# Two-level Strassen products in the first channel layer of the last batch

## The chip, the cores and the metric

The kernel runs on one NeuronCore of a Trainium2 chip. The metric is the device time of one execution in microseconds. Engine names are those of the profile: PE multiplies matrices, PEld loads its weights, DVE is VectorE, ACT is ScalarE, POOL is GpSimd, SP is SyncE, which issues nearly all DMAs.

## The reference

Inputs q, k and v have 4 batches, 8 heads, 768 positions and 64 columns a head. A sparse attention block makes x of 4 x 768 x 512, and this follows:

```python
X = np.fft.fft(x, axis=1)
X = np.fft.fft(X, axis=2)
u = x + np.real(X).astype(np.float32)
mu = np.mean(u, axis=-1, keepdims=True)
var = np.mean((u - mu) ** 2, axis=-1, keepdims=True)
un = (u - mu) / np.sqrt(var + 1e-06)
ch = np.maximum(un @ w_ch1, 0.0) @ w_ch2      # 512 -> 2048 -> 512
return (u + ch).astype(np.float32)
```

The change concerns `un @ w_ch1` of the last batch: 768 x 512 times 512 x 2048, all in float32.

## The kernel before

The program goes through the batches one after the other. For batch b it runs two channel layers and, beside them, the attention and the Fourier stage of batch b + 1. The last batch (b = 3) has nothing beside its channel layers: they are the last 145 us.

**Layer one** (`gen_hidden`, matmuls at L1377) makes the hidden activations in 16 tiles of 128 rows, taken in eight pairs j = 0 to 7. Rows of pair j come from the two halves of the hidden dimension, so a pair is a 2 x 2 block product: two tile rows, two halves of 384 positions, and a contraction over 512 that is cut in two halves of 256. It is done with Strassen's scheme in Winograd's form: seven products instead of eight. Each product contracts over 256, which is two matmuls (kk = 0, 1) of 384 columns. So a pair takes 14 matmuls. The seven left operands of a pair (A11, A12, S3, A22, S1, S2, S4) lie ready in DRAM as `dw1[j]` and come by `get_w1` into the three buffers of tag w1; the seven right operands (`u`, indices B11, T3, B21, B22, T1, T2, T4) are made on chip by `_right_sums` once per batch. Products go to three PSUM banks X, Y, Z (the profile's hx, hy, hz). ACT copies the first of each output block to h in SBUF (L1388, L1394, L1396), DVE adds the others (L571 is the helper `tt`), and a ReLU follows (DVE at L1383 for b > 0, ACT at L1407 for the last block).

**Layer two** (`gen_out`, matmuls at L1446) works in the same way on strips of 128 positions. Four left sums S1 to S4 are made by DVE from h (the profile's tile s), the right operands `dw2[j]` come by `get_w2`, and DVE adds the products ox, oy, oz to x. Each layer is cut in two parts, c = 0 and 1: four pairs in layer one, then a layer-two pass over these four (three strips i = 0 to 2), then the other four.

PSUM has eight banks: four of the tag "bank" (Fourier stage and channel layers) and four of the tag "attn" (attention).

**Order.** Generators yield after each piece, and `drive` takes pieces from several of them in turn. The program's instructions are then put on the engines' queues by priority, which is mostly program order; `tc.issue_after(mark)` puts an instruction behind a given one on its engine. Each engine works through its queue strictly in order, waiting at each instruction for what it needs. A buffer is reused when its readers are done.

The lines at which the last batch's channel layers begin are:

```python
most = chain(gen_hidden(b, 0), gen_out(b, 0), gen_hidden(b, 1))
...
drive((most, 44, 0), (gen_attention(b + 1) if b + 1 < B else iter(()), 80, 0))
last = gen_out(b, 1)
if b + 1 < B:
    drive((gen_fourier(b + 1), 22, 600), (last, 12, 0))
else:
    drive((last, 1, 0))
```

Of the kernel before, what the change touches and what calls it, by code (L numbers as in the profile page):

```python
# [9 lines left out]
FP = mybir.dt.float32  # L10
I32 = mybir.dt.int32
U32 = mybir.dt.uint32
AF = mybir.ActivationFunctionType
ALU = mybir.AluOpType
AX = mybir.AxisListType

P = 128
# [401 lines left out]
QB = 64  # L419
# [69 lines left out]
def _main_program(ctx, tc, q, k, v, moe_w_ch1, moe_w_ch2, out):  # L489


    nc = tc.nc
    B, H, S, D = q.shape
    DM = H * D
# [54 lines left out]
    def fetch(out, in_):  # L549

        ins = nc.sync.dma_start(out=out, in_=in_)
        if in_order[0]:
            tc.keep_in_program_order(ins)
        return ins.ins

    def abank(shape, name):
        return psum.tile(shape, FP, tag="attn", bufs=4, name=name)

    def bank(shape, name):
        return psum.tile(shape, FP, tag="bank", bufs=4, name=name)  # L560
# [9 lines left out]
    def tt(out, in0, in1, op):  # L570
        return nc.vector.tensor_tensor(out=out, in0=in0, in1=in1, op=op).ins  # L571
# [28 lines left out]
    def room(name):  # L600
        return bpool.tile([P, NC * 2 * S], FP, tag="room", name=name)
# [622 lines left out]
    def gen_fourier(b):  # L1224
# [117 lines left out]
        for t in range(NST):  # L1342
            half, i = divmod(t, HT)
            if b:
                normalise(half, i)
            ps = bank([P, 2, 2, P], f"unt_{b}_{t}")
            with tc.issue_after(marks[("av", 1, 0) if half else ("sc", 1, 0)]) if b == 0 else ExitStack():
                for d in range(NDT):
                    nc.tensor.transpose(ps[:, d // 2, d % 2, :], un[:, t, P * d:P * (d + 1)], ident)  # L1349
            ins = (nc.vector.tensor_copy if t % 2 and (b or half) else nc.scalar.copy)(  # L1350
                out=u[:, half:half + 3:2, :, P * i:P * (i + 1)], in_=ps)
            if t == NST - 1:
                marks["u"] = ins.ins
            yield
        _right_sums(tt, u.rearrange("p a k n -> p a (k n)"))
        wt["u", b] = u

    def gen_hidden(b, c):
        u = wt["u", b]
        js = range(NC * c, NC * (c + 1))  # L1360
        h = wt["h", b] = bpool.tile([P, NC, 2, S], FP, tag="h", name=f"h_{b}_{c}")
        for j in js:
            if 0 < j < NJ - 2:
                get_w1(b, j + 2)
            if (b, c) != (1, 0):
                get_w2(b, j)
            else:
                for i in ((0, 1), (2,), (3,), ())[j]:
                    get_w2(b, i)
            w = wt[1, b, j]  # L1370
            c11, c12 = h[:, j - NC * c, 0, 0:S2], h[:, j - NC * c, 0, S2:S]
            c21, c22 = h[:, j - NC * c, 1, 0:S2], h[:, j - NC * c, 1, S2:S]
            X, Y, Z = (bank([P, S2], f"h{n}_{b}_{j}") for n in "xyz")

            def product(ps, a, r, start, stop):
                for kk in range(2):
                    ins = nc.tensor.matmul(ps, w[:, a, kk, :], u[:, r, kk, :], start=start and kk == 0,  # L1377
                                           stop=stop and kk == 1, skip_group_check=True)
                marks["hidden", b] = ins.ins

            def relu(t):
                if b:
                    nc.vector.tensor_scalar(out=t, in0=t, scalar1=0.0, scalar2=None, op0=ALU.max)  # L1383
                else:
                    nc.scalar.activation(out=t, in_=t, func=AF.Relu)

            product(X, A11, B11, True, False)
            nc.scalar.copy(out=c11, in_=X)  # L1388
            product(Y, A12, B21, True, True)
            marks["dense"] = tt(c11, Y, c11, ADD)  # L1390
            some_sums(3 if (b, c) == (1, 0) and j else 0)
            yield
            product(X, S2_, T2, False, False)
            nc.scalar.copy(out=c12, in_=X)  # L1394
            product(Z, S1, T1, True, False)
            nc.scalar.copy(out=c22, in_=Z)  # L1396
            relu(c11)
            some_sums(3 if (b, c) == (1, 0) and j else 0)
            yield
            product(X, S3, T3, False, False)  # L1400
            marks["dense"] = tt(c22, X, c22, ADD)
            product(Z, S4, B22, False, True)
            marks["dense"] = tt(c12, Z, c12, ADD)
            some_sums(3 if (b, c) == (1, 0) and j else 0)
            yield
            product(X, A22, T4, False, True)
            nc.scalar.activation(out=c21, in_=X, func=AF.Relu)  # L1407
            relu(c22)
            relu(c12)
            issued.add(("h", b, j))  # L1410
            some_sums(3 if (b, c) == (1, 0) and j else 0)
            yield

    def gen_out(b, c):
        x, h = x_of[b], wt["h", b]
        js = range(NC * c, NC * (c + 1))
        if (b, c) == (0, 0):

            for t in range(NST):
                ps = bank([P, DM], f"o_{b}_{c}_{t}")  # L1420
                for n, j in enumerate(js):
                    for hf in range(2):
                        nc.tensor.matmul(ps, h[:, n, hf, P * t:P * (t + 1)], wt[2, b, j][:, 2 * hf:2 * hf + 2, :],  # L1423
                                         start=(n, hf) == (0, 0), stop=(n, hf) == (NC - 1, 1))
                    if n % 2 == 0:
                        yield
                tt(x[:, t, :], ps, x[:, t, :], ADD)
            issued.add(("o", b, c))
            return
        for i in range(HT):  # L1430
            t1, t2 = slice(P * i, P * (i + 1)), slice(S2 + P * i, S2 + P * (i + 1))
            left = {A11: h[:, :, 0, t1], A12: h[:, :, 1, t1], A22: h[:, :, 1, t2]}
            for s in (S1, S2_, S3, S4):
                left[s] = bpool.tile([P, NC, P], FP, tag="s", bufs=5, name=f"s{s}_{b}_{c}_{i}")
            a21 = h[:, :, 0, t2]
            tt(left[S1], a21, left[A22], ADD)
            tt(left[S2_], left[S1], left[A11], SUB)
            tt(left[S3], left[A11], a21, SUB)
            tt(left[S4], left[A12], left[S2_], SUB)
            X, Y, Z = (bank([P, HD], f"o{n}_{b}_{c}_{i}") for n in "xyz")  # L1440
            x11, x12 = x[:, i, 0:HD], x[:, i, HD:DM]
            x21, x22 = x[:, HT + i, 0:HD], x[:, HT + i, HD:DM]

            def product(ps, a, r, start, stop):
                for n, j in enumerate(js):
                    nc.tensor.matmul(ps, left[a][:, n, :], wt[2, b, j][:, r, :], start=start and n == 0,  # L1446
                                     stop=stop and n == NC - 1, skip_group_check=True)

            product(X, A11, B11, True, False)
            marks["dense"] = tt(x11, X, x11, ADD)  # L1450
            product(Y, A12, B21, True, True)
            marks["dense"] = tt(x11, Y, x11, ADD)
            yield
            product(X, S2_, T2, False, False)
            marks["dense"] = tt(x12, X, x12, ADD)
            product(Z, S1, T1, True, False)
            marks["dense"] = tt(x22, Z, x22, ADD)
            yield
            product(X, S3, T3, False, False)
            marks["dense"] = tt(x22, X, x22, ADD)  # L1460
            last = (b, c, i) == (B - 1, 1, HT - 1)
            if last:
                fetch(out=out[b, P * (HT + i):P * (HT + i + 1), HD:DM], in_=x22)
            product(Z, S4, B22, False, True)
            marks["dense"] = tt(x12, Z, x12, ADD)
            if last:
                fetch(out=out[b, P * i:P * (i + 1), :], in_=x[:, i, :])
            yield
            product(X, A22, T4, False, True)
            marks["dense"] = tt(x21, X, x21, ADD)  # L1470
            if NC * (c + 1) == NJ and not last:
                for t in (i, HT + i):
                    fetch(out=out[b, P * t:P * (t + 1), :], in_=x[:, t, :])
            elif last:
                fetch(out=out[b, P * (HT + i):P * (HT + i + 1), 0:HD], in_=x21)
            if i == HT - 1:
                issued.add(("o", b, c))
            yield


# [31 lines left out]
    def chain(*gens):  # L1512
        for gen in gens:
            yield from gen
# [51 lines left out]
    for b in range(B):  # L1566


        most = chain(gen_hidden(b, 0), gen_out(b, 0), gen_hidden(b, 1))
        if b == 0:  # L1570
            in_order[0] = False
            drive((most, 5, 0), (weights, 10, 0), (attn, 1, 0))
# [2 lines left out]
            drive((most, 44, 0), (gen_attention(b + 1) if b + 1 < B else iter(()), 80, 0))  # L1575
        last = gen_out(b, 1)
        if b + 1 < B:
            drive((gen_fourier(b + 1), 22, 600), (last, 12, 0))
        else:
            drive((last, 1, 0))  # L1580
# [53 lines left out]
```

## Time and profile before

| what | value |
|---|---|
| median of three runs | 793.5 us (792.02 to 793.65) |
| profiled execution, its own time | 790.53 us |
| its span in the profile | 788.6 us |
| PE busy | 776.1 us, 98% of the span |
| mean granted PE clock | 0.999 |
| last batch, layer one, c = 0 | 638.9 to 675.2 us |
| last batch, layer two, c = 0 | 675.2 to 711.5 us |
| last batch, layer one, c = 1 | 711.5 to 747.6 us |
| last batch, layer two, c = 1 | 747.6 to 784.4 us |

The profile describes one execution; its times are microseconds from the start of the span, and the execution takes about 2 us more than the span. A float32 matmul of the program appears as two records of PE and two weight loads of PEld. A line of a group of instructions names source line, engine, operation, output<-inputs, shapes and count; then busy time and mean duration in ns; then the idle time of the engine ahead of them and what ended it. A table by stretches gives the busy time of each engine in a stretch, with the number of instructions, the granted clock, the DMA share and GB/s.

### The profile page before, as it was taken

What the parts mean: (1) busy time and instruction counts of PE and PEld (TensorE: products, weight loads), DVE (VectorE), ACT (ScalarE), POOL (GpSimd) and SP (SyncE); (2) the same over time, 40 slices, a digit from 0 to 9 for tenths busy, and PEclk for the clock granted to TensorE, in tenths of its full rate; (3) what the DMA queues carried; (4) which work ended last, traced back from release to release, by engine and by line L of the source; (5) the groups of instructions that cost most, each with busy time, mean ns of one, the idle gap of its engine ahead of it and who ended that gap; (6) DMA issues with size and microseconds to landing.
All of it is one profiled execution on the core that took longest, in us unless ns stands there. A gap on an engine that the chain in (4) does not pass through costs nothing.

```text
span 788.6 us, 14351 instructions
## 1 busy us (share of the span) xinstructions
PE 776.1 (98%) x5920; PEld 562.9 (71%) x5920; DVE 491.2 (62%) x1017; ACT 224.1 (28%) x491; POOL 49.2 (6%) x87
## 2 busy tenths in 40 slices
PE   9999999999999999999999999999999999999997
PEld 6778455445588866787578866788569865886686
DVE  5899978697889566652759545552667623533352
ACT  3565656236536022100236012200136012001200
POOL 0000000000000030200310020300220000000000
PEclk9999999999999999999999999999999999999999
DMA  9999887796855279965442169611513163106001
GB/s 214 184 266 237 206 275 196 242 260 221 232 161 155 49 231 261 204 103 177 154 144 87 54 209 212 184 55 31 223 44 134 54 220 134 47 0 234 0 28 57
DMA packets 133353, 121.82 MB, mean 154 GB/s; under 512 B 94464, under 2 KB 114912, under 8 KB 133088
## 3 DMA queue, kind: packets, MB, share of 16 engines
q1 hardware_dynamic: 132160, 118.53, 53.9%
q0 software_dynamic: 576, 2.10, 0.8%
q8 instruction: 48, 0.79, 0.4%
q10 hardware_dynamic: 544, 0.20, 0.1%
q14 instruction: 25, 0.20, 0.1%
HBM read 97.22 MB, written 23.59 MB: 153 GB/s over the span
## 4 chain that ended last, share of the span: by engine, by line
PE 87%; DVE 9%; ACT 1%; issue 1%; DMA 1%; POOL 0%; SPq 0%; DVEq 0%; POOLq 0%
PE hx L1377 19%; PE ox L1446 18%; PE hz L1377 10%; PE oz L1446 9%; PE hy L1377 5%; PE oy L1446 5%; PE o L1423 4%; PE y L1258 3%; PE sc L793 2%; PE mx L1217 2%; PE av L829 1%; PE av L834 1%; PE qk L718 1%; DVE x L571 1%; PE unt L1349 1%
## 5 line engine op out<-in xcount | busy, mean ns | idle before, releaser
L1377 PE MATMUL hx<-u,w 128*128 128x384 f32 x512 | 185.4, 491 | 1.5 <-ACT h L1394 0.7
L1377 PEld LDWEIGHTS hx<-u,w 128*128 128x128 f32 x512 | 94.9, 190 | 70.3 <-ACT p L800 3.8
L1377 PE MATMUL hz<-u,w 128*128 128x384 f32 x256 | 93.7, 487 | 0.2 <-DVE u L571 0.2
L1446 PE MATMUL oz<-w,s 128*128 128x256 f32 x336 | 81.3, 380 | 0.0
L1446 PE MATMUL ox<-w,s 128*128 128x256 f32 x336 | 80.1, 380 | 0.0
L1446 PE MATMUL ox<-w,h 128*128 128x256 f32 x336 | 79.6, 381 | 0.0
L571 DVE TENSOR_TENSOR x<-ox,x 128x256 f32<-128x256 f32 x84 | 35.5, 423 | 66.2 <-PE ox L1446 65.9
L1377 PEld LDWEIGHTS hz<-u,w 128*128 128x128 f32 x256 | 48.4, 190 | 34.1 <-DVE u L571 0.8
L1446 PEld LDWEIGHTS ox<-w,h 128*128 128x128 f32 x336 | 63.1, 190 | 10.8 <-issue 1.2
L1446 PEld LDWEIGHTS oz<-w,s 128*128 128x128 f32 x336 | 63.3, 190 | 8.9 <-DVE x L571 0.4
L1446 PEld LDWEIGHTS ox<-w,s 128*128 128x128 f32 x336 | 63.2, 190 | 9.0 <-DVE x L571 0.3
L1388 ACT COPY h<-hx 128x384 f32<-128x384 f32 x32 | 15.3, 479 | 187.1 <-PE hx L1377 187.1
L571 DVE TENSOR_TENSOR h<-hy,h 128x384 f32<-128x384 f32 x32 | 17.8, 557 | 48.4 <-PE hy L1377 48.2
L1377 PE MATMUL hy<-u,w 128*128 128x384 f32 x128 | 46.8, 487 | 0.6 <-DVE h L571 0.6
L571 DVE TENSOR_TENSOR h<-hx,h 128x384 f32<-128x384 f32 x32 | 17.8, 556 | 44.1 <-PE hx L1377 43.9
L1423 PE MATMUL o<-w,h 128*128 128x512 f32 x96 | 42.3, 595 | 0.7 <-DVE w L571 0.7
L1407 ACT ACTIVATE h<-hx 128x384 f32<-128x384 f32 x32 | 15.7, 490 | 88.3 <-PE hx L1377 88.2
L1446 PE MATMUL oy<-w,h 128*128 128x256 f32 x168 | 40.1, 380 | 0.0
L571 DVE TENSOR_TENSOR x<-oz,x 128x256 f32<-128x256 f32 x42 | 17.8, 424 | 30.4 <-PE oz L1446 30.1
L1377 PEld LDWEIGHTS hy<-u,w 128*128 128x128 f32 x128 | 24.1, 190 | 16.9 <-DVE h L571 0.7
L1446 PEld LDWEIGHTS oy<-w,h 128*128 128x128 f32 x168 | 31.8, 190 | 4.4
L1423 PEld LDWEIGHTS o<-w,h 128*128 128x128 f32 x96 | 18.0, 190 | 22.7 <-issue 20.7
(167 smaller groups left out, 1072.8 us busy)
## 6 DMA issues: line engine op xcount, KB each, us to landing
w<-dw SPq DMA_DIRECT2D x44, 896.0 KB, 5.7
words<-in_moe_w_ch_dram SPq DMA_DIRECT2D x32, 512.0 KB, 5.7
dw<-w SPq DMA_DIRECT2D x12, 896.0 KB, 7.5
vw<-in_v_dram SPq DMA_DIRECT2D x47, 192.0 KB, 6.1
out_dram<-x SPq DMA_DIRECT2D x23, 256.0 KB, 2.0
vb<-in_v_dram SPq DMA_DIRECT2D x24, 192.0 KB, 6.8
kn<-in_k_dram SPq DMA_DIRECT2D x9, 384.0 KB, 6.1
qn<-in_q_dram SPq DMA_DIRECT2D x9, 384.0 KB, 7.6
```

Source lines behind the costliest of these rows:

```text
L571: return nc.vector.tensor_tensor(out=out, in0=in0, in1=in1, op=op).ins
L718: nc.tensor.matmul(ps[D * e:D * (e + 1), s:S2:HT], src[:, e, h, s, :], ident, start=True, stop=True)
L793: ins = nc.tensor.matmul(ps[h][r:r + 64, i, :], kt[rows, o:o + 64], qt[rows, o:o + BLOCK], start=True, stop=True)
L829: nc.tensor.matmul(av[r][32 * j:32 * (j + 1), t, :], p[rows, h, i - NB2 * h, :], vw[rows, i, :], start=(t == 0), stop=False, skip_group_ch ...
L834: ins = nc.tensor.matmul(av[r][:, t:t + HT + 1:HT, :], pm[rows, P * t:P * (t + 1)], vs[rows], start=False, stop=(t == HT - 1), skip_group_ ...
L1217: nc.tensor.matmul(out, y[:, g], table, start=False, stop=True, skip_group_check=True)
L1258: nc.tensor.matmul(y, fgs[b][par][:, st, P * g:P * (g + 1)], fs[par][:, g % 2, st, :], start=(st == 0), stop=(st == n - 1))
L1377: ins = nc.tensor.matmul(ps, w[:, a, kk, :], u[:, r, kk, :], start=start and kk == 0, stop=stop and kk == 1, skip_group_check=True)
L1388: nc.scalar.copy(out=c11, in_=X)
L1407: nc.scalar.activation(out=c21, in_=X, func=AF.Relu)
L1423: nc.tensor.matmul(ps, h[:, n, hf, P * t:P * (t + 1)], wt[2, b, j][:, 2 * hf:2 * hf + 2, :], start=(n, hf) == (0, 0), stop=(n, hf) == (NC ...
L1446: nc.tensor.matmul(ps, left[a][:, n, :], wt[2, b, j][:, r, :], start=start and n == 0, stop=stop and n == NC - 1, skip_group_check=True)
```

## The change

In the last batch, tile pairs 2 and 3, 4 and 5, and 6 and 7 of layer one are each taken together, and the products of such a couple get a second level of the same scheme. An outer product (one of the seven) has, for the two tile pairs, two tile rows of 128, two contraction halves of 128 and two column halves of 192: again a 2 x 2 block product, so seven inner matmuls of 192 columns in place of eight (four matmuls of 384 columns). Tile pairs 0 and 1 stay as they were, and so does the last outer product of each part c (four matmuls of 384 columns). That leaves 19 outer products with seven inner matmuls.

The inner scheme is done partly in PSUM. Inner product 1 goes to t; ACT copies t into f's first half, and inner product 2 is added to that by PE. Inner product 6 is added to t; ACT copies t into f's second half, and 3 is added there. Inner product 7 is added to t; ACT copies t to g, and 4 is added there. Product 5 goes to z, beside t in one bank. So f holds two of the four output blocks, g the third, and the fourth is t + z, which DVE adds. The inner matmuls of neighbouring outer products are interleaved in a fixed order (`events`), so that other matmuls stand between a copy and its use.

The outer scheme's sums, in SBUF, also change form: U2 is the first product plus S2·T2, U3 is U2 plus S3·T3, and product Z is kept in its own tile zs and added to two blocks by DVE. ReLUs of finished blocks run on POOL; the ones that finish late run on ACT.

The second level needs its own operand sums. DVE makes the right ones (`right_halves`, eight instructions, during tile pairs 0 and 1) and the left ones (`left_halves`, four per couple: for tile pairs 2 and 3 during the last strip of batch 2's layer two, for the others during strips 1 and 2 of layer two, c = 0). They use the attention's buffers, a buffer of tag x and the big one of tag room. The block of tile pair 3, and later 7, is loaded into two former attention buffers.

```diff
+                    if b == B - 1:
+                        nc.tensor.matmul(ps[:, d // 2, d % 2, :], un[:, t, P * d:P * (d + 1)], ident, start=d == 0,
+                                         stop=d == NDT - 1, is_transpose=True, skip_group_check=True)
...
-    def gen_hidden(b, c):
+    def gen_hidden(b, c, js=None):
...
-            if 0 < j < NJ - 2:
+            if 0 < j < NJ - 2 and b < B - 1:
                 get_w1(b, j + 2)
...
+    def right_halves(u, uu):
+        q = [[u[:, :, kk, H2 * n:H2 * (n + 1)] for n in range(2)] for kk in range(2)]
+        for r in (slice(0, 4), slice(4, 7)):
+            b11, b12, b21, b22 = (q[kk][n][:, r] for kk in range(2) for n in range(2))
+            t1, t2, t3, t4 = (uu[:, i, r] for i in range(4))
+            for a in ((t1, b12, b11), (t2, b22, t1), (t3, b22, b12), (t4, b21, t2)):
+                with tc.issue_after(marks["dense"]):
+                    tt(*a, SUB)
+                yield
...
+    def one_sum(b, c, i):
+        if (b, c, i) == (B - 2, 1, HT - 1) and "last" not in queue:
+            queue["last"] = left_halves(B - 1, 2, 6)
+        if i and queue.get("last"):
+            with tc.issue_after(marks["dense"]):
+                tt(*queue["last"].pop(0))
...
+    def load_fourth(j):
+        wide, rest = four[0]
+        with tc.issue_after(marks["load"]):
+            fetch(out=wide, in_=dw1[j][:, 0:6])
+        fetch(out=rest, in_=dw1[j][:, 6])
+        wt[1, B - 1, j] = four[0]
+
+    def gen_two(b, c, pairs):
+        order = (("11", A11, B11), ("U2", S2_, T2), ("11+", A12, B21), ("U3", S3, T3), ("Z", S1, T1), ("21", A22, T4),
+                 ("12", S4, B22))
+        todo = [(j,) + o for j in pairs for o in order]
+        last = todo.pop()
+        N = len(todo)
+        events = [(7 * n + s, n, m) for n in range(N)
+                  for s, m in ((0, 1), (4, 2), (5, 6), (9, 7), (10, 3), (13, 4), (15, 5))]
+        events += [(7 * N + s, N, m) for s, m in ((0.5, (0, 0)), (4.5, (1, 0)), (8.5, (0, 1)), (8.6, (1, 1)))]
...
+        def finish(n):
+            j, name = todo[n][:2]
+            late = j == pairs[-1]
+            if name == "11+":
+                relu(view(j, 0, 0), False)
+            elif name == "21":
+                relu(view(j, 1, 0), late)
+            elif name == "12":
+                relu(view(j, 0, 1), late)
+            elif name == "Z":
+                add(view(j, 0, 1), view(j, 0, 1), tmp[j], ADD)
+                add(view(j, 1, 1), view(j, 1, 0), tmp[j], ADD)
+                relu(view(j, 1, 1), False)
+
+        def step(n, m):
+            j, name, a, r = todo[n]
+            if m == 1:
+                ps = bank([P, 2, H2], f"t_{b}_{c}_{n}")
+                slots[n] = ps[:, 0], ps[:, 1], abank([P, 2, H2], f"f_{b}_{c}_{n}"), abank([P, H2], f"g_{b}_{c}_{n}")
+            z, t, f, g = slots[n]
+            o = {1: t, 6: t, 7: t, 2: f[:, 0], 3: f[:, 1], 4: g, 5: z}[m]
+            with tc.issue_after(marks["two"]) if "two" in marks else ExitStack():
+                marks["two"] = nc.tensor.matmul(o, left(j, a, m), rhs(r, m), start=m in (1, 5), stop=m in (2, 3, 4, 5, 7),
+                                                skip_group_check=True).ins
+            if m in (1, 6, 7):
+                nc.scalar.copy(out={1: f[:, 0], 6: f[:, 1], 7: g}[m], in_=t)
+            if m not in (3, 4, 5):
+                return
+            out, src = target(n)
+            fv = f.rearrange("p i t -> p (i t)")
+            if m == 3:
+                nc.scalar.copy(out=out[:, 0], in_=fv) if src is None else add(out[:, 0], fv, src[:, 0], ADD)
+            elif m == 4:
+                nc.scalar.copy(out=out[:, 1, 0:H2], in_=g) if src is None else add(out[:, 1, 0:H2], g, src[:, 1, 0:H2], ADD)
+            else:
+                o0, o1 = out[:, 0, H2:S2], out[:, 1, H2:S2]
+                if src is None:
+                    add(o0, z, o0, ADD)
+                    in_turn(nc.vector.tensor_copy, out=o1, in_=t)
+                    add(o1, z, o1, ADD)
+                else:
+                    if name in ("11+", "12", "21"):
+                        add(out[:, :, H2:S2], z[:, None, :].to_broadcast([P, 2, H2]), out[:, :, H2:S2], ADD)
+                    else:
+                        add(o0, z, o0, ADD)
+                        add(o1, z, src[:, 1, H2:S2], ADD)
+                    add(o1, t, o1, ADD)
+                finish(n)
...
+    def last_layers(b):
...
+        hidden, two = gen_hidden(b, 0, range(2)), gen_two(b, 0, (2,))
+        pieces = right_halves(wt["u", b], right[b])
+        for i in range(7):
+            next(hidden)
+            for _ in range(2 if i == 0 else 1):
+                next(pieces)
+            yield
...
+        next(two)
+        yield from hidden
+        get_w1(b, 4)
+        get_w1(b, 5)
+        yield from two
+        get_w1(b, 6)
+        load_fourth(7)
+        queue["last"] = left_halves(b, 4, 7) + left_halves(b, 6, 6)
+        last, two = gen_out(b, 0), gen_two(b, 1, (4, 6))
+        for _ in range(11):
+            next(last)
+            yield
+        next(two)
+        yield from last
...
+            one_sum(b, c, i)
             yield
...
-        most = chain(gen_hidden(b, 0), gen_out(b, 0), gen_hidden(b, 1))
+        most = chain(gen_hidden(b, 0), gen_out(b, 0), gen_hidden(b, 1)) if b < B - 1 else last_layers(b)
...
+            if b == B - 2:
+                prepare_last()
             drive((gen_fourier(b + 1), 22, 600), (last, 12, 0))
```

The call `one_sum` stands at the end of each of the four pieces of a strip in `gen_out`. `in_turn` keeps the DVE instructions of `gen_two` in the order in which they are made.

## The prediction

> **What bounds the kernel now.** I read the busy shares first, then a table of four stretches (the last batch's two channel layers, each in two halves), then what waits there, then the instruction prices.
>
> ```profile
> PE 776.1 (98%) x5920; PEld 562.9 (71%) x5920; DVE 491.2 (62%) x1017; ACT 224.1 (28%) x491; POOL 49.2 (6%) x87
> ```
>
> ```profile
> core 0: us, PE busy (x) PEld busy (x) DVE busy (x) ACT busy (x) POOL busy (x), PEclk, DMA share, GB/s
> 638.90:675.20 36.30, 36.30 (x115) 21.46 (x114) 11.66 (x27) 7.22 (x15) 0.00 (x0) 1.00 0.52 190
> 675.20:711.50 36.30, 36.30 (x170) 31.96 (x169) 15.56 (x32) 0.49 (x1) 0.00 (x0) 1.00 0.09 28
> 711.50:747.60 36.10, 36.10 (x114) 21.26 (x113) 11.68 (x26) 7.22 (x15) 0.00 (x0) 1.00 0.32 126
> 747.60:784.40 36.80, 36.29 (x169) 31.59 (x167) 15.97 (x33) 0.49 (x1) 0.00 (x0) 1.00 0.11 41
> ```
>
> The first and third stretches are `gen_hidden`, the two others `gen_out`. PE has no gap, its clock is full, DVE works a third of the time, ACT a fifth, POOL not at all. So a matmul less saves its time and a wait on PE costs its time; DVE, ACT and POOL cost something only where PE waits for them. A program matmul in f32 stands as two records. In the chain of waits:
>
> ```profile
> 672.67 1.29 PE hz L1377 x4
> 673.96 1.29 PE hx L1377 x4
> 675.25 1.73 PE ox L1446 x8
> ...
> 676.97 1.73 PE oy L1446 x8
> ```
>
> Four records of 384 columns take 1.29 us: 0.645 us per matmul, and layer two starts with no gap. Eight records of 256 columns take 1.73, so 0.432 per matmul. The halved matmul has 192 columns; the Fourier stage has one of 193:
>
> ```profile
> 587.53 3.10 PE L1258 MATMUL y<-fs,fold 128*128 128x193 f32 x18
> 590.47 0.82 PE L1262 MATMUL y<-fs,fold 128*128 128x193 f32 x4
> ```
>
> 18 records in 2.94 us are 163.3 ns each. 384, 256 and 193 columns lie on one line, 2.5 ns + 0.833 ns per column: 192 columns give **0.325 us per matmul**. The weight load, 190 ns long in the groups, doesn't set that rate. Other prices:
>
> ```profile
> L571 DVE TENSOR_TENSOR x<-ox,x 128x256 f32<-128x256 f32 x84 | 35.5, 423 | 66.2 <-PE ox L1446 65.9
> L571 DVE TENSOR_TENSOR h<-hy,h 128x384 f32<-128x384 f32 x32 | 17.8, 557 | 48.4 <-PE hy L1377 48.2
> L571 DVE TENSOR_TENSOR u<-u 128x768 f32<-128x768 f32 x8 | 7.6, 954 | 0.0
> ```
>
> ```profile
> 588.06 0.34 ACT L1263 COPY yt<-y 128x192 f32<-128x192 f32 x1 [1.14 <-PE y L1258]
> 588.28 0.35 ACT L1264 COPY yt<-y 128x192 f32<-128x192 f32 x1
> 677.52 0.42 DVE L571 TENSOR_TENSOR x<-ox,x 128x256 f32<-128x256 f32 x1
> 677.86 0.68 DVE L571 TENSOR_TENSOR s<-h 128x512 f32<-128x512 f32 x1
> ```
>
> DVE: 1.05 ns per column, so an add of 192 columns out of PSUM lasts 0.356 us. An instruction without a wait starts about 0.08 before the end of the one ahead (677.52 to 677.86); one that waits for it starts 0.03 after. ACT copies 192 columns in 0.34. In the timeline ACT starts 0.20 after the last column of a matmul, DVE 0.20 to 0.27; I take 0.27.
>
> **What the Trainium skill says.** "TensorE: Matmul & The Clock Gate", section "Back-to-back issue gap", gives a matmul alone N/2.4 + 2.5 ns; the trace agrees on the 2.5 and has twice the slope for an f32 record. "PSUM — Partial Sum Buffer", "The four PSUM rules": a ScalarE write leaves the written-bits alone, and a matmul without the start flag adds onto it where they are set. The change rests on this; no run here shows it. "SBUF — State Buffer", "Who interferes with whom": VectorE contends with a reading GpSimd when both of its inputs are in SBUF. POOL is idle in all four stretches above, so they don't test it.
>
> **The change, part by part.**
>
> Matmuls. The three couples of tile pairs had 84 matmuls of 384 columns: 84 x 0.645 = 54.18 us. Now 19 of the 21 outer products take seven of 192 columns each and two keep their four of 384: 133 x 0.325 + 8 x 0.645 = 48.39. Gain **5.79 us**, all on PE's path.
>
> The round trip. Per outer product PE writes t, ACT copies t to f's first half, PE adds onto both; twice more for f's second half and for g. In the built order at least three other matmuls, 0.975 us, stand between. Needed: 0.20 + 0.34 + 0.03, and 0.16 because the weight load precedes its matmul (587.37 against 587.53 in the timeline): 0.73. Slack 0.24, so 57 trips cost nothing in the steady part. At each of the two starts only one matmul, 0.325, stands ahead of the second trip: 0.73 - 0.325 = 0.4, twice: **0.8 us**.
>
> VectorE per outer product: U2, U3: one add of 384 and four of 192, about 1.8 us; the others 1.1 to 1.7, against seven slots of 0.325 = 2.275 on PE. Z is the exception: three instructions of 192, then two sums of 768. Count from PE's last column of Z: DVE starts at 0.27; three instructions to 1.29; sums to 3.14; the next product ("21") adds to f by 3.73, to g by 4.00, finishes at 4.98.
>
> Consequence inside the second half: g of product "12" takes the bank that f of "21" leaves (built program). It can be copied from 3.75 on instead of 2.8; PE needs it at 3.58 (eleven slots) and gets it at 3.75 + 0.34 + 0.19 = 4.28: **0.7 us**, once, as only couple (4, 5) is followed by another.
>
> Consequence at the change to layer two, twice. After Z, PE has 4 x 0.325 + 3 x 0.645 = 3.24, then `ox` and `oy` of layer two, 1.73 each: 6.69, and then needs S1. `oy` takes the bank of "21", free at 4.98, wanted at 4.96: 0.1 with the weight load. DVE adds the two last products by 5.92; ACT, with four ReLUs of 0.49 in its queue from 5.05, ends at 6.77; S1 (684 ns in the rows s<-h) ends at 7.48. With 0.13 for hand-over and weights PE starts at 7.6 instead of 6.69: **0.9 us, 1.8 in both**. Late next is S2, at about 8.6, but PE has three `oz` matmuls (1.3) till 8.9.
>
> Edits at nothing, with their cover. Left sums of couple (2, 3) (four of 954 ns) go behind drained banks in the last `gen_out` strip of batch 2; the tightest is 0.42 + 0.95 within the 1.73 of a product. Those of the other couples likewise, in strips where DVE then has about 10 of 12.1 us. Right sums (four of 954, four of about 0.75 us: 6.8) go into two tile pairs of 9.03 that hold 2.75 of DVE each; three in a row end at 6.6, when the add that PE's next `hx` waits for can begin at 6.7. Without cover each would cost PE up to its own length. POOL takes the early ReLUs; the price of 768 columns isn't in the trace, between 0.76 (its memset of 768) and 2.0 us (twice the 1.0 of its 384 tensor_tensor), wanted three us or more later. The transposes of the last batch change only flags: order and count stay.
>
> DMAs. The block of tile 3 comes as two loads (786 and 131 KB) on SP, ahead of the Fourier tables. SP is idle from 560 to 568 us and the attention buffers are free since 519 (its last av matmul starts at 518.5), so the first lands before the table's turn, the second is 0.3 us of issue. Tile 7's blocks and `get_w1` 4 to 6 are issued 20 us and more before use. Behind them on SP stand only second-layer weights, wanted later still.
>
> Sum: -5.79 + 0.8 + 0.7 + 1.8 = **-2.5 us**. The profiled execution has a span of 788.6 and took 790.53, so 788.0; it is 3.0 under the median of 793.5, from which the same step gives **791.0 us**. Unknown sizes: the starts 0.5 to 1.0, the bank wait 0 to 0.9, a change of layer 0.3 to 1.5 (no overlap between DVE instructions). Ends: stalls of 1.1 to 4.9, so 788.8 to 792.6.
>
> **The rivals.** (a) The handed-over work hides: DVE runs the 192-column adds faster than the line says, and only the starts cost. For: DVE's overlap is known only for longer instructions. Against: Z's two sums of 768 have a row. -5.0: 788.5. (b) Each DVE instruction waits for the last: layers 1.5 each, bank 0.8, starts 0.9: 4.7, net -1.1: 792.4. For: many in-place adds. Against: the f and g adds write different columns. (c) **Slower**: ACT's round trip, at the banks that PE adds onto, is longer than three slots. Break-even with the limit of 0.2% is at 57 x 0.073 = 4.2 us beyond the stalls above, a trip of 1.05 us. At 1.1 it costs 7.1: +4.6, 798.1. For: no trace of before shows a matmul onto a bank that ACT wrote, and ACT's 384-column copies stand in the same queue. Against: 0.24 of slack over measured parts.
>
> **How the numbers follow.** My case 0.50 (own range 789.9 to 792.1), (a) 0.17, (b) 0.18, (c) 0.12, a mishap of another kind 0.03. 0.2% is 1.6 us, about what a measurement of this kernel tells from no change: limits 791.9 and 795.1. Faster: 0.17 + most of my case (0.42) + 0.03 of (b) = 0.62; the same: 0.08 + 0.15 = 0.23; slower: (c) and the mishap, 0.15. The range 788.2 to 794.5 leaves out (c) and the mishap.
>
> **What would show it.** Right: 192-column records 163 ns apart; PE idle in the last 150 us about 3 us, on waits for ACT at two starts, for ACT behind DVE once, for DVE at `oz` twice. Wrong: PE waits for ACT in every product (c), or no wait at `oz` (a), or more than 1.5 us there (b). A PE idle before the last batch's layers would refute the cover of the sums.

## The result and the profile after

The changed kernel takes 792.0 us, median of 14 runs (790.4 to 795.6); the kernel before 793.6, median of 14 (790.9 to 795.5). The ratio is 0.9986, 95% interval 0.9969 to 1.0003. Measured again with more runs it is 0.9989, interval 0.9976 to 1.0002. So the program is about 1 us faster by these ratios, which the times of whole programs don't tell from nothing: both intervals reach past 1. The profiled execution took 790.64 us with a span of 787.8 (before: 790.53 and 788.6).

The profile tells more than the time, since the length of the last batch repeats to 0.01 us from one profile of a kernel to the next (shown below). First the busy times of the page after, then the four stretches of the last batch (layer one and layer two of the first channel half, then of the second), each cut at its own borders:

```profile
PE 772.1 (98%) x6034; PEld 576.5 (73%) x6034; DVE 525.0 (67%) x1087; ACT 238.3 (30%) x544; POOL 66.3 (8%) x95
```

```profile
core 0: us, PE busy (x) PEld busy (x) DVE busy (x) ACT busy (x) POOL busy (x), PEclk, DMA share, GB/s
640.10:674.80 34.70, 34.63 (x149) 25.86 (x150) 21.38 (x45) 10.91 (x30) 2.14 (x1) 1.00 0.48 175
674.80:712.50 37.70, 37.10 (x172) 32.09 (x171) 24.87 (x46) 2.15 (x5) 2.12 (x1) 1.00 0.13 49
712.50:745.50 33.00, 32.34 (x190) 30.70 (x189) 22.48 (x54) 14.63 (x46) 10.55 (x5) 1.00 0.27 110
745.50:783.10 37.60, 36.89 (x169) 31.52 (x167) 18.46 (x40) 1.84 (x4) 2.13 (x1) 1.00 0.11 38
```

Layer one is shorter, layer two longer. The exact borders are starts in the timeline: first `hx`, first `ox`, last sum of VectorE. One `t` matmul, 0.33, stands inside the first `ox` stretch and is counted to the layer one that it belongs to:

| us | before | after | difference | gain of the matmuls alone | lost |
|---|---|---|---|---|---|
| layer one, first half | 36.22 | 34.73 | -1.49 | 1.83 | 0.34 |
| layer two, first half | 36.26 | 37.36 | +1.10 | 0 | 1.10 |
| layer one, second half | 36.12 | 33.35 | -2.77 | 3.96 | 1.19 |
| layer two, second half | 36.46 | 37.56 | +1.10 | 0 | 1.10 |
| last batch | 145.06 | 143.00 | **-2.06** | 5.79 | 3.73 |

The last column is the whole question. Before, PE waited for no other engine in this part; now the list of waits (engine, line, what it waited for: total, times, longest) has

```profile
PE oy L1661 <- DVE h L1504: 0.7, 2, 0.4
PE g L1548 <- ACT g L1551: 0.6, 1, 0.6
PE oz L1661 <- DVE s L571: 0.4, 2, 0.2
PEld oy L1661 <- PE ox L1661: 1.5, 2, 0.7
PEld oz L1661 <- DVE s L571: 1.2, 2, 0.6
PEld g L1548 <- ACT g L1551: 0.9, 1, 0.9
PEld t L1548 <- ACT f L1551: 0.7, 2, 0.4
```

A weight load waits in its matmul's place, so a PEld line and a PE line of one tile are the same stop, seen from two instructions; they are not added. They stand at five places, all of them places that the prediction named: two starts (`t`), one bank (`g`), and two changes of layer (`oy`, then `oz`).

A stop costs more than its wait. Here is the first start. Without a stop, the two records of a matmul of 192 columns take 0.325 until the next matmul begins:

```profile
659.16 0.49 PE L1548 MATMUL t<-u,w 128*128 128x192 f32 x2
...
659.71 0.30 PEld L1548 LDWEIGHTS t<-halves,w 128*128 128x128 f32 x2 [0.36 <-ACT f L1551]
659.72 0.59 PE L1548 MATMUL t<-halves,w 128*128 128x192 f32 x2
...
660.14 0.49 PE L1548 MATMUL f<-u,s 128*128 128x192 f32 x2
```

PE stands 0.23 (659.485 to 659.715), and then the matmul takes 0.43 (659.72 to 660.14) instead of 0.325, as its second record begins 0.10 late. The weight load, which starts 0.16 ahead of its matmul in the steady part (659.00 for the matmul at 659.16), starts together with it after the stop. The same 0.10 follows the stops of `g` and `oz`; after that of `oy`, whose weight load starts 0.03 ahead, it is 0.07. With this the account closes: 0.34 at each start, 0.75 + 0.10 at `g`, 1.10 at each change of layer, together 3.73. Between the stops the chain of waits is TensorE alone.

How a change of layer goes, from the timeline (start, length), second half, rows of the weight loads and of other lines left out:

```profile
741.90 0.49 PE L1548 MATMUL t<-halves,vw 128*128 128x192 f32 x2
...
742.84 0.36 DVE L1504 TENSOR_TENSOR zs<-t,zs 128x192 f32<-128x192 f32 x1 [1.94 <-PE t L1548]
...
743.96 1.83 DVE L1504 TENSOR_TENSOR h<-h,zs 128x768 f32<-128x768 f32 x2
...
745.46 1.89 PE L1661 MATMUL ox<-w,h 128*128 128x256 f32 x8
...
746.63 0.94 DVE L1504 TENSOR_TENSOR h<-t,h 128x384 f32<-128x384 f32 x2
...
747.72 1.97 PE L1661 MATMUL oy<-w,h 128*128 128x256 f32 x8 [0.37 <-DVE h L1504]
...
749.16 0.69 DVE L571 TENSOR_TENSOR s<-h 128x512 f32<-128x512 f32 x1 [0.33 <-ACT h L1591]
...
749.90 1.56 PE L1661 MATMUL oz<-w,s 128*128 128x256 f32 x6 [0.22 <-DVE s L571]
```

Read it downward: product Z's last column leaves PE at 742.23; VectorE's three instructions of 192 columns, then the two sums of 768, hold the sums of product "21" back until 747.57, and `oy`, which takes the bank of "21", starts 0.54 after `ox` has ended (747.72, and 745.458 + 1.727 = 747.185). The operand sum S1 comes after the ReLUs of the last products, and `oz` starts 0.46 late (749.45 wanted): 0.07 is the late second record of `oy` (eight records in 1.97, against 1.89 of `ox`), 0.38 the wait for S1. The second record of `oz` is late by 0.10. The product with S2 behind it waits for nothing.

### The profile page after: what moved, and what is told of

The parts are those of the page before. It is cut to its first block, busy times and chain, and to the rows that moved or that the text cites. A ratio compares the mean times of both kernels' runs of the same rounds, so it can differ in the third digit from the quotient of the medians.

```text
span 787.8 us, 14784 instructions
## 1 busy us (share of the span) xinstructions
PE 772.1 (98%) x6034; PEld 576.5 (73%) x6034; DVE 525.0 (67%) x1087; ACT 238.3 (30%) x544; POOL 66.3 (8%) x95
## 4 chain that ended last, share of the span: by engine, by line
PE 85%; DVE 9%; ACT 3%; issue 1%; DMA 1%; POOL 0%; DVEq 0%; ACTq 0%; POOLq 0%
PE ox L1661 17%; PE hx L1381 17%; PE oz L1661 9%; PE hz L1381 8%; PE o L1638 4%; PE hy L1381 4%; PE oy L1661 4%; PE y L1258 3%; PE t L1548 3%; PE mx L1217 2%; PE sc L793 2%; PE av L829 2%; PE av L834 1%; PE f L1548 1%; PE ss L811 1%
## 5 line engine op out<-in xcount | busy, mean ns | idle before, releaser
L1381 PE MATMUL hx<-u,w 128*128 128x384 f32 x416 | 151.4, 492 | 1.6 <-ACT h L1398 0.8
L1381 PEld LDWEIGHTS hx<-u,w 128*128 128x128 f32 x416 | 76.7, 190 | 57.7 <-ACT p L800 3.7
L1381 PE MATMUL hz<-u,w 128*128 128x384 f32 x208 | 76.1, 487 | 0.0
L1381 PEld LDWEIGHTS hz<-u,w 128*128 128x128 f32 x208 | 39.4, 190 | 27.1
L1392 ACT COPY h<-hx 128x384 f32<-128x384 f32 x26 | 12.5, 479 | 147.2 <-PE hx L1381 147.2
L1381 PE MATMUL hy<-u,w 128*128 128x384 f32 x104 | 38.1, 488 | 0.0
L574 POOL TENSOR_TENSOR vb<-vb 96x512 f32<-96x512 f32 (+2 forms) x20 | 20.7, 1037 | 181.3 <-DMA vb<-in_v_dram 115.0
L571 DVE TENSOR_TENSOR h<-hy,h 128x384 f32<-128x384 f32 x26 | 14.5, 557 | 29.9 <-PE hy L1381 29.7
L1411 ACT ACTIVATE h<-hx 128x384 f32<-128x384 f32 x26 | 12.7, 490 | 65.7 <-PE hx L1381 65.6
L571 DVE TENSOR_TENSOR h<-hx,h 128x384 f32<-128x384 f32 x26 | 14.5, 556 | 23.7 <-PE hx L1381 23.4
```

The source lines that it names most:

```text
L574: return nc.gpsimd.tensor_tensor(out=out, in0=in0, in1=in1, op=op).ins
```

## The experiments

All lengths are of the last batch, from the first `hx` to the start of VectorE's last sum: 145.06 before, 143.00 after. The theory: the 5.79 us are there, and stops at five places give 3.7 back: the unfilled start (twice), a bank that VectorE frees late (`g`), and VectorE's late sums at a change of layer (twice). The rivals: the trips over ScalarE, VectorE's load as a whole, disturbance of the stages ahead. Each edit below stands in one profiled execution; the last batch repeats well enough for that.

**A22·T4 third in layer two**, in row block 0 of the last batch, so that PE has 1.73 us of work that needs no operand sum:

```
  product(Y, A12, B21, True, True)
+ V = bank([P, HD], ...)
+ product(V, A22, T4, True, True);  x21 += V
  product(X, S2_, T2, ...)
...
- product(X, A22, T4, False, True)
  x21 += X
```

> Edit: in layer two of the last batch, row block 0 of each channel half, the product A22*T4 is taken out of its place at the end and issued third, into a bank of its own, and VectorE adds it to x21 beside the old sum: four matmul pairs (about 1.73 us of TensorE work) that need no operand sum stand ahead of the products with S1 and S2. Theory (the change lost its gain at the layer changes, because VectorE arrives late with the operand sums S1 and S2 and with the bank of oy): the wait before oz goes, the wait of 0.5 before oy stays, so layer two takes about 37.0 in each half against 37.5 in the changed kernel and 36.3 in the kernel before; last batch from the first hx to the last matmul 142.9 to about 141.9. Rival (layer two is longer because its own matmuls run slower or VectorE is short of time all along it): both lengths stay at 37.5.

Measured: 141.65. The stop before `oz` is gone in both halves. Layer two takes 37.19 - 0.33 = 36.86 in the first half (0.50 less) and 36.71 in the second (0.85 less); in the second the stop before `oy` shrank too, from 0.54 to 0.18, because VectorE began Z's first sum 0.35 earlier there, of which below. The rival (a slower layer two all along) falls.

**One Z sum on GpSimd:**

```
- add(view(j, 0, 1), view(j, 0, 1), tmp[j], ADD)
+ nc.gpsimd.tensor_tensor(out=view(j, 0, 1), in0=view(j, 0, 1), in1=tmp[j], op=ADD)
```

> Edit: of the two sums of 768 columns with which a product Z ends, the one into row half (0,1) goes to GpSimd (three instructions in all), so VectorE has 0.96 us less ahead of the sums of product 21. Theory (VectorE's 1.8 us of Z sums is what holds bank f at the mid wait and the bank of oy): the wait of g before the second couple falls from 0.75 to 0.2 or less, the waits before oy (0.5) go, the operand sums of layer two come 0.9 earlier and the waits before oz (0.5 each) go: 142.9 to about 140.3, layer two about 36.5 in each half. Rival (GpSimd's sum of two inputs takes over 4 us, or slows VectorE [...]): product 12 then waits for it on VectorE and layer one gets longer, 142.9 to 144 or more. Rival (the waits come from ScalarE's copies, not from VectorE): no change, 142.9.

Measured: 141.62, half of what was expected. The stop of `g` in the middle is gone, and both before `oy`: it was VectorE's queue that held those banks, not the copies. But the stop before `oz` stayed, and one of 0.29 came behind it, where the product with S2 begins:

```profile
DVE s L571 <- POOL h L1524: 1.4, 2, 0.7
PEld oz L1661 <- DVE s L571: 1.4, 2, 0.8
```

S1 needs A22, whose ReLU stands on GpSimd behind the new sum (2.59 us each, 128x768) and after it takes its own 2.12. VectorE is earlier and waits 0.7 for GpSimd: one late input in place of another.

**Start three matmuls earlier:**

```
+ if i == 6: next(two)     # one piece earlier (second half: i == 10)
  next(hidden)
...
  next(two)
+ next(two)
```

> Edit: the first three inner matmuls of each of the two parts are issued one piece earlier, the first ahead of the second-last piece of the work before, the next two ahead of its last piece (1.3 us in layer one, 1.7 us in layer two), so that the ScalarE trip of the third lies beside that piece. Theory (the two waits for ScalarE of 0.39 at the starts are an unfilled pipeline): both go, 142.9 to about 142.1, all else unchanged. Rival (the start waits for the bank or for an operand, not for the trip): the wait moves ahead of the first inner matmul and nothing is gained, 142.9.

Measured: 142.48, a gain of 0.52. Both waits for the trip are gone. It is less than the 0.36 to 0.39 that the list shows for each, since a weight load that runs ahead stops 0.16 before its matmul would have: PE itself lost 0.34 at each start, as shown above. Of these 0.67, 0.16 came back: the second record of an early `f` matmul begins 0.10 late in the first half and 0.07 in the second.

**The two edits on TensorE's order without GpSimd's sum:**

> Edit: the two edits of the order on TensorE (A22*T4 third, the start three matmuls earlier) without the sum on GpSimd. Theory (A22*T4 covers the late operand sums, but only a shorter VectorE queue frees bank f and the bank of oy): the mid wait (0.6) and the waits before oy (0.4 each) stay, last batch 143.0 less 1.2 to 2.0, so 141.0 to 141.8, against 139.4 with the sum on GpSimd. Rival (the sum on GpSimd adds nothing once TensorE's order is changed): 139.4 to 140.0.

Measured: 141.16. The stop of `g` (0.6) and the stop before `oy` (0.4) in the first half stay; in the second half `oy` stops 0.18, as in the run with A22·T4 third alone. Moving the sum to GpSimd is the edit that frees these banks in time.

**All three edits:**

> Edit: the three edits before this one together (A22*T4 third at each layer change, one Z sum on GpSimd, the start three matmuls earlier). Theory (the change is worth 5.79 us of TensorE time and loses about 3.7 of it at five places, which these edits fill): last batch 142.9 to between 139.2 and 139.8, time 2.3 to 3.0 us under the changed kernel measured beside its own stage, about 5 us under the kernel before, ratio to the kernel before 0.992 to 0.995. Rival (the rest of the loss lies elsewhere, or each filled wait comes back behind the next): 141 or more, ratio 0.997 or more.

Measured: 139.43, and 789.09 us, median of 7 runs (786.7 to 791.1); ratio to the kernel before 0.9942, interval 0.9921 to 0.9963. It beats both kernels (it was not timed beside the changed one, but its interval lies wholly below that one's 0.9976 to 1.0002). Its four stretches:

```profile
644.10:678.60 34.50, 34.50 (x151) 25.90 (x150) 21.30 (x45) 10.67 (x30) 3.60 (x2) 1.00 0.48 175
678.60:714.90 36.30, 36.30 (x171) 32.09 (x170) 24.48 (x46) 2.48 (x6) 3.23 (x2) 1.00 0.13 50
714.90:747.10 32.20, 32.20 (x191) 30.91 (x190) 21.53 (x54) 14.40 (x45) 14.60 (x7) 1.00 0.29 115
747.10:783.60 36.50, 36.40 (x169) 31.70 (x167) 18.07 (x40) 1.86 (x4) 3.20 (x2) 1.00 0.11 40
```

No wait of PE is left in the list, layer two takes 36.3 and 36.5 as before the change, and 5.63 of the 5.79 us are there; the missing 0.16 are the same two late records of `f` as with the earlier start alone. So the loss lay at those five places and nowhere else. GpSimd's late ReLU costs nothing here: S1 waits for it (0.74), and A22·T4 covers that.

**Longer trips over ScalarE**, by one and by two more copies of the same tile into unused columns ahead of each of the 57:

```
  if m in (1, 6, 7):
+     for _ in range(1):     # 2 in the second run
+         nc.scalar.copy(out=room_end[:, 0:H2], in_=t)
      nc.scalar.copy(...)
```

> Edit to the changed kernel: ahead of each of the 57 copies of 192 columns on ScalarE one more copy of the same tile into unused columns of SBUF, so each trip from TensorE over ScalarE and back takes about 0.21 us longer. Theory (three matmuls of 0.325 between the two ends of a trip leave it a slack of about 0.25, so the trips of the changed kernel cost nothing): last batch, from the first hx to the start of VectorE's last sum, stays near 143.0, at most 144. Rival (the trips are the bound of the two-level part already, by their length or by ScalarE's total work): a good part of 57 times 0.21 shows, 147 to 155.

> Edit: two such copies more ahead of each of the 57, about 0.42 us longer trips. Theory (slack of 0.25): the trip now ends last and TensorE waits some 0.17 in one to two of the three trips of each product, 19 products: last batch 143.0 plus 3 to 10, waits of PE for ScalarE in every product. Rival (the trips have far more slack, so ScalarE is no danger to this design): 143.0 to 144.

Measured: 143.87 and 153.39. One copy delays a trip by 0.22 (starts 664.99 and 665.20 in the timeline) and costs 0.87 in all (layer one +0.35 and +0.52): 0.59 of it at the two starts, 0.26 at one `g` of the second half. The other trips bear it. Two delay it by 0.57, not 0.42 (starts 664.91 and 665.48): of two copies to one place, the second starts 0.35 after the first, where a copy to another place starts 0.22 after. Now PE stops in every product; its waits for ScalarE:

```profile
PEld g L1549 <- ACT g L1554: 6.4, 19, 0.6
PEld f L1549 <- ACT f L1554: 4.3, 18, 0.4
PEld t L1549 <- ACT f L1554: 4.1, 13, 1.0
```

Layer one is 3.85 and 7.10 longer, 10.95 over 19 products, the starts included: 0.58 per product. In the steady part each of the three trips costs 0.16 to 0.17 (more around product Z), and 0.10 of that is the late second record. How much slack a trip has, the starts of the changed kernel tell: one matmul of 0.325 stands in a trip there and 0.23 is lost, so a trip needs 0.56, and three matmuls, 0.975, leave 0.42. That agrees with both runs: 0.22 more fits in, 0.57 doesn't. The last batch is 10.4 longer, just over the 3 to 10 expected, by the longer delay and because all three trips of a product stop. This run doesn't separate the length of a trip from ScalarE's total work, which the expectation of the run before it named too: ScalarE is busy 28.96 of the 32.00 us from 722 to 754. The mechanism of the slower rival exists, then, but about 0.4 us per trip away.

**Second half alone:**

```
- hidden, two = gen_hidden(b, 0, range(2)), gen_two(b, 0, (2,))
+ hidden = gen_hidden(b, 0, range(4))
```

> Edit: the tile pair couple (2,3) is computed by one level again, only the couples (4,5) and (6,7) of the second channel half by two. Theory (gain and loss belong to each half by itself: the second half gained 2.77 in layer one and lost 1.10 at its change to layer two): first half as in the kernel before (36.2 and 36.3), the second as in the changed kernel (33.4 and 37.6), last batch about 143.4 against 145.1 before and 143.0 in the changed kernel. Rival (the halves disturb each other, by banks or by VectorE's load in the first layer two, where the operand sums of couples (4,5) and (6,7) lie): the second half differs from the changed kernel's by over 0.3.

Measured: 143.04; the first half as before (36.22 and 36.26), layer one of the second as in the changed kernel (33.34), its layer two 37.22 instead of 37.56. About 143.4 was expected, and the second half differs from the changed kernel's by 0.34, which is what the rival said: the halves are not independent. What differs is where VectorE began Z's first sum: 0.60 after the start of Z's last matmul, in the changed kernel 0.94 (742.84 - 741.90), and so the stop before `oy` was 0.19 instead of 0.54. Neither banks nor VectorE's load are shown to be the reason. So as it stands couple (2, 3) brings almost nothing (143.00 against 143.04): it gains 1.49 in layer one, 1.10 goes back at its change of layer, and without it the second half is 0.34 shorter.

**The changed kernel again, and the kernel before twice more:**

> The changed kernel again, with nothing edited. Theory (its stages fix 2.06 of gain, and what differs ahead of the last batch is scatter between executions): last batch 143.0 within 0.1, the first hx of the last batch at another time than 640.0 by up to 4 us either way, ratio to the kernel before 0.996 to 0.999. Rival (the longer program itself delays the stages before): the first hx again 1 us or more after the kernel before's 638.9 in every execution, ratio 0.999 to 1.002.

> The kernel before, with nothing edited, profiled once more. Theory (the stages ahead of the last batch scatter from execution to execution, in both kernels alike, and the change has no part in it): the first hx of the last batch stands anywhere between 638 and 644, as in the nine profiles of the changed kernel and its edits (638.7 to 644.1), and the last batch takes 145.1. Rival (the longer program delays what stands ahead of it): the first hx stands at 638.9 within 0.5, as in the one profile of this kernel so far.

> As for the run before this one: theory, a first hx that differs from that run's by up to 5; rival, 638.9 within 0.5 again. The last batch 145.1 in both.

Measured: changed kernel 143.00, first `hx` at 638.7. Kernel before 145.07 and 145.07, first `hx` at 645.6 and 643.2, against 638.9 in its first profile; 645.6 lies even outside the 638 to 644 expected. The last batch repeats to 0.01; what stands ahead of it scatters by 6.7 us in one and the same kernel, three times the effect looked for. Of the 6.7, 4.9 us had been lost by the first `hx` of batch 0 (85.8 against 80.9). From 80 to 120 us the granted clock was 0.96 in the later profile with 645.6 and 1.00 in the first one, but most of the 4.9 were lost ahead of that, and their cause stays open. The rival, that the longer program delays the stages ahead, has the traces against it. All that the change edits ahead of the last batch (operand sums, loads, transposes) lies behind the first `hx` of batch 2's second half, and from there to the last batch it is 88.76 us in the kernel before (550.10 to 638.86) and 88.76 in the changed one (551.26 to 640.02); the other profiles of the two have 88.76 to 88.78. The scatter lies ahead of that. A small share of the rival can't be excluded there: the stage saves 2.06, 0.26%, which lies inside the first interval and 0.02% outside the second.

## Why the prediction was right, and where it was off

The sum of steps was -2.5 us, the last batch gave -2.06, the medians -1.6 (14 runs each) and -1.0 (27 and 22 runs). The faster-by-over-0.2% case that I gave most of the chance is not what the ratio shows; 0.9986 is within 0.2%. Step by step:

- **Matmuls, 5.79.** Right: 5.63 remain once every stop is filled. The records of 192 columns begin 162.5 ns apart, as predicted (659.16 and 659.32 for the `t` matmul ahead of the first stop).
- **The trip, slack 0.24, free in the steady part.** Free it is; the slack is about 0.4, the need 0.56 instead of 0.73. The copy between banks takes 303 ns where I took 340 from a copy into SBUF, and the 0.16 for the weight load does not belong in the trip. The Trainium skill, "PSUM — Partial Sum Buffer", section "The four PSUM rules", has a matmul without the start flag add onto what ScalarE wrote where the written-bits are set; 57 such trips now run, and the trace shows their time (0.56), not the adding itself.
- **Starts, 0.8 in both.** Nearly right, in part by luck: 0.67. The wait is 0.56 - 0.325 = 0.23 each, less than the 0.4 taken, and the 0.10 of the late second record, which I did not have, makes up for much of that.
- **Bank of `g`, 0.7, once.** Right: wanted at 728.70, begun at 729.45, 0.75, and 0.10 for the late second record.
- **Change of layer, 0.9 each.** Sum nearly right, parts not: 1.10 each. I had 0.1 before `oy` and 0.8 before `oz`; the waits are 0.54 and 0.38, and the late second records 0.07 and 0.10. S2 is just in time, as I had put it. The term that was mis-sized is VectorE's start after Z: 0.27 after the last column was taken, 0.62 was found (742.84 - 742.225), so everything behind it moved by 0.35. S1 did not move so far, as there the ReLUs on ScalarE end last.
- **Edits at nothing.** Right: the stretch that holds the first left sums, the loads and the transposes is as long as before (88.76), and no wait of PE for the right sums or the later left sums is in the list. GpSimd's ReLU of 768 columns takes 2.13 us, slightly over the upper bound that I gave; in the changed kernel nobody waits for it.
- **What the sum left out.** The late second record after each stop, seven times, takes 0.67 of the 3.73 that were lost. With these included, two starts, one bank and two changes of layer make 0.67 + 0.86 + 2.20 = 3.73, and nothing remains.

Rival (a), only the starts cost, fell at `oy`, `g` and `oz`. Rival (b), 1.5 per change of layer, is too high there (1.10 lies nearer to my 0.9) and in the starts, and near at the bank (0.8, and 0.86 measured). Rival (c), the long trip, did not happen, and the copies showed how near it was.

The point itself, 791.0, is the median of three runs less 2.5; that the median of the changed kernel came within 1.0 us of it says little where single runs lie 5 us apart. The chance for "faster" rested on a limit of 1.6 us under a predicted effect of 2.5. The 0.4 us that the steps missed left 2.06, still over the limit; the rest of the shortfall in the ratio lies within its interval.

## What to carry to other kernels

A cheaper algorithm on a full engine is paid in its own stage and charged at the borders: at the start, where the pipeline is empty, at the end, where the next stage wants what the busier helper finishes last, and where a bank passes on. In this kernel each stop also cost up to 0.10 beyond its wait, where the weight load no longer ran ahead. Price the helper's queue from the last product to the first use, and have work that needs none of it ready for that gap; here one product moved forward covered 0.5 us of late operands at either change of layer. Moving a sum to an idle engine shortens one queue and lengthens another: see what stands behind it there before expecting the whole gain.

## What was not expected of the hardware

- VectorE began Z's first sum 0.94 us after the start of Z's last matmul in most changes of layer, but 0.60 between the two couples of the second half in all ten kernels and profiles that have both, and 0.60 at the second change of layer of four kernels (A22·T4 third, with and without the earlier start; the sum on GpSimd; second half alone), with the same instructions around it. The changed kernel gave 0.94 in both of its profiles. It is not one more matmul that VectorE waits for: by the semaphore records of the traces its wait for TensorE ends 0.55 after that start in both kinds (742.45 in the changed kernel, 745.05 with A22·T4 third), and the sum begins 0.40 later in the one and 0.04 later in the other. What sets it stays open.
- GpSimd's sum of 768 columns with two inputs takes 2.59 us, its ReLU with one input 2.13. VectorE's sum of 768 beside the former kept its 0.96 (0.956 in the changed kernel), and so did the shorter ones. The Trainium skill, "SBUF — State Buffer", section "Who interferes with whom", has a VectorE instruction with two inputs in SBUF contend with a GpSimd instruction that reads SBUF; VectorE's, which began 0.04 first (742.77 against 742.82), showed nothing of it. GpSimd's sum of 384 columns takes 1.00 in the kernel before, so by proportion 2.0 would be the estimate for 768. Whether the rest of the 2.59 is a wait, no run tells, as VectorE's sum stands beside it each time.
